# A kernel of spectral filter and gated MLP: two early activation columns moved ahead of the first weights, those weights in smaller loads and on two queues, and a row table moved back

## The chip, the cores and the metric

The kernel runs on one core of a Trainium2 chip. The metric is the device time of one execution in microseconds (us). A run of a kernel is repeated in rounds beside the kernel before on the same chip; medians are quoted. Ratios are computed as the mean time of one kernel's fast runs over that of the other's of the same rounds, so they are not quite the ratio of the medians quoted beside them. Brackets after a ratio hold its 95% interval. A core's execution can fall into a slower state.

Engine names in the profile: PE is TensorE's matmuls, PEld TensorE's weight loads, DVE VectorE, ACT ScalarE, POOL GpSimd, SPq and ACTq the queues of instructions on SyncE and ScalarE that issue loads (a load is moved afterwards by the core's 16 DMA engines).

## The reference

The output is the sum of the input, of a spectral filter of its layernorm, and of a gated MLP of the same layernorm:

```python
x = A_x                                    # 1 x 2048 x 512, bf16
xn = _layernorm(x, axis=-1)
# A: irfft2(rfft2(xn) * (w_r + 1j*w_i)), cast to bf16
# B: g = xn @ w_gate; u = xn @ w_up        # 512 x 1792 each
#    h = gelu_tanh(g) * u; h @ w_down      # 1792 x 512
return x + A(xn) + B(xn)
```

## The kernel before

The 2048 rows of x are 16 "columns" of 128 rows. TensorE needs x normalised and transposed (`xnT`), so column 0 must land, be normalised on VectorE, be transposed on TensorE and be copied out before the first gate matmul can run. Meanwhile TensorE runs dummy matmuls on a zero tile. The first gate and up matmuls work on columns 0 and 1 and on 512 of the 1792 weight columns (512 KB for each of `Wg_sb` and `Wu_sb`). All loads go out on SyncE in this order:

```python
pin(load_x(0, 1))                          # 128 KB, column 0
pin(load_x(1, 1))                          # 128 KB, column 1
nc.sync.dma_start(out=idx_t[:], ...)       # row table: 12 bytes to each partition, 1.5 KB
load_w(Wg_sb, 0, 512)                      # 512 KB, packets of 1 KB
load_w(Wu_sb, 0, 512)                      # 512 KB
load_x(2, 2)                               # 256 KB, packets of 2 KB
load_w(Wg_sb, 512, 1024)
load_w(Wu_sb, 512, 1024)
load_x(4, 2)
load_x(6, 2)
load_w(Wg_sb, 1024, DF)
load_w(Wu_sb, 1024, DF)
load_x(8, 2)
# [... more columns and constants]
for k in range(37):
    pin(nc.tensor.matmul(sp_ps[:, :P], lhsT=spin[:], rhs=spin[:], start=True, stop=True))
```

A list scheduler written in the kernel puts the rest in order, from guesses of when data lands. Its guesses touch the order of instructions only; the real waits are on semaphores.

```python
LAND = {0: 2.9, 1: 3.6, 2: 8.4, 3: 8.4}             # columns of x
WG_LAND = [6.3] * 4 + [10.2] * 4 + [13.2] * 6       # gate weights, by 128 columns
WU_LAND = [7.4] * 4 + [11.7] * 4 + [15.2] * 6
# [...]
# the first gate block, in two halves (rows 0-255 and 256-511 of the weights):
if k == 0:
    g = add("PE", occ / 2, lambda: mm_half(0), [xT_op[0, 0]], key=1000, acq=("G",), t_min=WG_LAND[0])
    g = add("PE", occ / 2, lambda: mm_half(1), [xT_op[0], g], key=1000.1, lat=occ / 2 + 0.3)
# [...]
u = split("u_ps", "U", Wu_sb, 1003.1 if k == 2 else 1000.5 + k, WU_LAND, (2, m, 1)[k] if k < 3 else m)
```

## Time and profile before

| | before |
|---|---|
| median time, us | 178.76 (178.62 to 179.22) |
| span of the profiled execution, us | 176.7 |
| TensorE busy in it, us | 171.1 (97%) |
| first gate matmul starts, us | 6.13 |
| first up matmul starts, us | 7.60 |
| third weight group starts (second gate group), us | 8.51 |

First two lines of the page: the busy time of each engine with its share of the span, and TensorE's busy tenths in 40 equal slices.

```profile
PE 171.1 (97%) x1127; PEld 96.2 (54%) x1145; DVE 116.1 (66%) x255; ACT 95.9 (54%) x170; POOL 17.2 (10%) x38
...
PE   7899999999999999999999999999999999999993
```

The busy time by stretch of the same kernel: the stretch, its length, then busy us and number of instructions of PE, PEld, DVE, ACT and POOL, the granted TensorE clock, the busy share of the DMA engines, and GB/s.

```profile
0.00:5.00 5.00, 3.62 (x38) 3.46 (x39) 2.10 (x10) 1.87 (x3) 0.69 (x6) 1.00 0.46 131
5.00:6.13 1.13, 0.85 (x10) 0.51 (x11) 1.07 (x5) 1.10 (x2) 0.00 (x0) 1.00 1.08 379
6.13:14.00 7.87, 7.68 (x106) 7.19 (x107) 4.71 (x12) 3.34 (x6) 0.97 (x2) 1.00 1.04 360
14.00:24.00 10.00, 9.95 (x80) 7.73 (x80) 9.82 (x24) 5.09 (x8) 1.73 (x4) 1.00 1.06 353
24.00:60.00 36.00, 35.79 (x218) 18.50 (x221) 24.06 (x44) 27.95 (x50) 13.81 (x26) 1.00 0.66 147
```

TensorE works without gaps of note from 7.6 us to the end, so an opening that is shorter by half a microsecond is half a microsecond won.

The opening, in the timeline: start, duration, engine, line, operation, tiles, shape, count of merged instructions, and in brackets the idle time before it with what ended it.

```profile
2.17 0.43 SPq L277 DMA_DIRECT2D Wg_sb<-in_B_w_gate_dram  x1
2.65 0.51 SPq L277 DMA_DIRECT2D Wu_sb<-in_B_w_up_dram  x1
2.96 0.69 DVE L339 BATCH_NORM_STATS2 stats<-x_t 128x6 f32<-128x512 bf16 x1 [1.94 <-DMA x_t<-in_A_x_dram]
...
5.59 0.29 DVE L354 COPY xnT<-tp 128x256 bf16<-128x256 bf16 x1
...
6.13 0.90 PEld L498 LDWEIGHTS <-Wg_sb 128*128 128x128 bf16 x16 [0.41 <-DMA Wg_sb<-in_B_w_gate_dram]
6.13 1.07 PE L498 MATMUL g_ps<-xnT,Wg_sb 128*128 128x128 bf16 x16 [0.24 <-DMA Wg_sb<-in_B_w_gate_dram]
...
7.60 1.07 PE L490 MATMUL u_ps<-xnT,Wu_sb 128*128 128x128 bf16 x16 [0.18 <-DMA Wu_sb<-in_B_w_up_dram]
...
8.51 1.06 PE L490 MATMUL g_ps<-xnT,Wg_sb 128*128 128x128 bf16 x16
```

Column 0 is ready at 5.88 (the copy at 5.59 takes 0.29), TensorE has done its last dummy matmuls at 5.89, and the gate matmul waits 0.24 us from there for its weights. The up matmul waits 0.18 for its own. So 0.4 us of waiting for loads can be seen, and that is what the change goes for.

### The profile page before, as it was taken

The numbers are of one execution on the slowest core, as the hardware profiler recorded it, in microseconds if no ns is written. First come the engines' busy times: TensorE is split into PE (matmuls) and PEld (weight loads), VectorE is DVE, ScalarE is ACT, GpSimd is POOL, SyncE is SP. The second block draws the span as 40 slices with busy tenths as digits, with TensorE's granted clock in tenths as the row PEclk, the third lists the DMA queues.
The fourth block names the chain that finished last, engine by engine and source line by source line (L and its number), as shares of the span: only waits on it lengthen the run. The fifth ranks groups of instructions, "written<-read, shape, count | busy, mean of one in ns | idle before, by whom it ended". The sixth has DMA issues, their size and how long they took to land.

```text
span 176.7 us, 3114 instructions
## 1 busy us (share of the span) xinstructions
PE 171.1 (97%) x1127; PEld 96.2 (54%) x1145; DVE 116.1 (66%) x255; ACT 95.9 (54%) x170; POOL 17.2 (10%) x38
## 2 busy tenths in 40 slices
PE   7899999999999999999999999999999999999993
PEld 7698845455544554555555445454444445444463
DVE  3588999987333699979899999643516325345333
ACT  4442489799736988898899965362112111211200
POOL 1020340506760000000000000000000000000000
PEclk9999999999999999999999999999999999999999
DMA  3999999234718702211211510200122221221212
GB/s 98 345 382 377 375 183 151 59 73 64 253 32 269 269 2 58 59 31 34 59 25 36 152 46 15 59 0 4 59 89 89 82 71 61 89 89 60 82 41 59
DMA packets 21871, 19.35 MB, mean 110 GB/s; under 512 B 8480, under 2 KB 20000, under 8 KB 21856
## 3 DMA queue, kind: packets, MB, share of 16 engines
q1 hardware_dynamic: 21440, 17.84, 36.2%
q0 software_dynamic: 416, 1.32, 2.4%
q8 instruction: 9, 0.15, 0.4%
q14 instruction: 6, 0.05, 0.1%
HBM read 13.38 MB, written 2.10 MB: 88 GB/s over the span
## 4 chain that ended last, share of the span: by engine, by line
PE 94%; DMA 3%; SPq 1%; issue 1%; DVE 0%
PE u_ps L490 27%; PE y_ps L817 27%; PE g_ps L490 27%; DMA Wu_sb<-in_B_w_up_dram 3%; PE yp L768 2%; PE gp L738 2%; PE bp L577 2%; PE dp L635 2%; PE y_ps L821 2%; PE ep L644 2%; SPq L273 0%; PE tp L351 0%; SPq L277 0%; SPq L284 0%; DVE y_sb L824 0%
## 5 line engine op out<-in xcount | busy, mean ns | idle before, releaser
L490 PE MATMUL u_ps<-xnT,Wu_sb 128*128 128x512 bf16 (+2 forms) x264 | 56.5, 340 | 0.5 <-DMA Wu_sb<-in_B_w_up_dram 0.2
L490 PE MATMUL g_ps<-xnT,Wg_sb 128*128 128x512 bf16 (+2 forms) x252 | 55.9, 349 | 0.2
L817 PE MATMUL y_ps<-Wd_sb,hT 128*128 128x512 bf16 (+2 forms) x246 | 50.6, 355 | 0.3
L508 DVE TENSOR_TENSOR hT<-u_ps,ge 128x512 bf16<-128x512 f32 x56 | 38.4, 688 | 18.1 <-PE u_ps L490 11.1
L503 ACT ACTIVATE ge<-g_ps 128x512 bf16<-128x512 f32 x56 | 33.7, 601 | 24.2 <-PE g_ps L490 20.8
L490 PEld LDWEIGHTS <-Wu_sb 128*128 128x128 bf16 x272 | 24.8, 98 | 21.0 <-DMA Wu_sb<-in_B_w_up_dram 0.4
L817 PEld LDWEIGHTS <-hT 128*128 128x128 bf16 x252 | 23.2, 98 | 22.4
L490 PEld LDWEIGHTS <-Wg_sb 128*128 128x128 bf16 x256 | 24.0, 98 | 20.6
L774 ACT CAST yf<-yp 128x512 bf16<-128x512 f32 x16 | 9.3, 586 | 40.5 <-PE yp L768 40.5
L824 DVE TENSOR_TENSOR y_sb<-y_ps,y_sb 128x512 bf16<-128x512 f32 (+2 forms) x18 | 11.1, 631 | 30.0 <-PE y_ps L821 30.0
L649 ACT CAST E<-ep 64x512 bf16<-64x512 f32 x32 | 18.5, 579 | 1.4 <-PE ep L644 1.0
L339 DVE BATCH_NORM_STATS2 stats<-x_t 128x6 f32<-128x512 bf16 x16 | 10.4, 674 | 2.6 <-DMA x_t<-in_A_x_dram 2.6
L452 ACT ACTIVATE xn<-x_t,nb,rstd 128x512 bf16<-128x512 bf16 x12 | 9.5, 812 | 1.0 <-POOL nb L370 1.0
L547 ACT CAST ds<-dp 128x512 bf16<-128x512 f32 x16 | 9.2, 597 | 0.8 <-PE dp L635 0.8
L547 ACT CAST Gs<-gp 128x512 bf16<-128x512 f32 x16 | 8.7, 591 | 0.6 <-PE gp L738 0.5
L547 ACT CAST Bs<-bp 128x512 bf16<-128x512 f32 x16 | 8.3, 608 | 0.5 <-PE u_ps L490 0.5
L780 DVE TENSOR_TENSOR lv<-yf 128x512 bf16<-128x512 bf16 x16 | 6.1, 422 | 1.5 <-ACT yf L774 0.6
L768 PEld LDWEIGHTS <-Gs 128*128 128x128 bf16 x64 | 4.8, 98 | 3.5
L787 DVE TENSOR_TENSOR yt<-lv 128x512 bf16<-128x512 bf16 x16 | 6.1, 422 | 0.3
L768 PE MATMUL yp<-CT,Gs 128*128 128x128 bf16 x64 | 6.0, 219 | 0.1
L821 PE MATMUL y_ps<-yt,RI_t 128*128 128x512 bf16 (+2 forms) x18 | 6.1, 355 | 0.0
L559 DVE TENSOR_TENSOR A<-xn 128x1024 bf16<-128x1024 bf16 x8 | 5.2, 676 | 1.0 <-ACT xn L452 1.0
(65 smaller groups left out, 118.2 us busy)
## 6 DMA issues: line engine op xcount, KB each, us to landing
F<-F SPq DMA_DIRECT2D x32, 64.0 KB, 2.0
y_sb<-in_A_x_dram SPq DMA_DIRECT2D x16, 128.0 KB, 2.1
out_dram<-y_sb SPq DMA_DIRECT2D x15, 128.0 KB, 1.7
x_t<-in_A_x_dram SPq DMA_DIRECT2D x7, 256.0 KB, 8.7
Wd_sb<-in_B_w_down_dram SPq DMA_DIRECT2D x1, 1792.0 KB, 7.7
Wg_sb<-in_B_w_gate_dram SPq DMA_DIRECT2D x2, 512.0 KB, 6.4
Wu_sb<-in_B_w_up_dram SPq DMA_DIRECT2D x2, 512.0 KB, 6.1
Wg_sb<-in_B_w_gate_dram SPq DMA_DIRECT2D x1, 768.0 KB, 10.2
```

Source lines behind the costliest of these rows:

```text
L339: V.bn_stats(out=st[:], in_=x_t[:, c, :])
L452: xn_op[c] = add("ACT", 0.72, lambda c=c: A.activation(out=xn[:, c, :], in_=x_t[:, c, :], func=AF.Identity, bias=nb[:, c:c + 1], scale=rst ...
L490: T_.matmul(b[name][:, f], lhsT=W_[:, e, (f0 + f) * P:(f0 + f + 1) * P], rhs=rhs[:, e, :], start=(e == 0), stop=(e == NE - 1))
L503: A.activation(out=b["ge"][:], in_=b["g_ps"][:], func=AF.Gelu_apprx_tanh)
L508: V.tensor_tensor(out=hT_of(sb, f0, m, o, w), in0=b["u_ps"][:], in1=b["ge"][:], op=ALU.mult)
L547: A.copy(out=o, in_=i)
L649: A.copy(out=b["E"][64 * h:64 * h + 64, r], in_=b["ep", h][64 * r:64 * r + 64])
L768: T_.matmul(t[:, q], lhsT=late["G"][:, q, c0 + j], rhs=IQ[q], start=(q == 0), stop=(q == 3), skip_group_check=True)
L774: A.copy(out=b["yf"][:, j], in_=b[j][:])
L817: T_.matmul(b[o][:], lhsT=hT_of(sb, f, 1, cl * P, P)[:, 0], rhs=Wd_sb[:, f, o:o + w], start=(f == 0), stop=False)
L821: T_.matmul(b[o][:], lhsT=late["RI"][:, c, :], rhs=late["yt"][:, c, o:o + w], start=False, stop=True)
L824: V.tensor_tensor(out=b["y"][:, o:o + w], in0=b[o][:], in1=b["y"][:, o:o + w], op=ALU.add)
```

## The change

The intent: bring columns 2 and 3 in while the weights would only start slowly; let two hardware queues feed the DMA engines with the first gate weights, in quarters, so that the first matmuls may start on a part; hold ScalarE's issues back behind a longer VectorE write to the same tile (a memset of zeros that the loads must wait for), so that they do not overtake column 0; move a tiny row table out of the front; use larger loads later on; and adapt the scheduler's guesses. The core of the diff (the rest moves the same statements into a function `opening()` that is called at the head of the schedule):

```diff
+        nc.vector.memset(Wg_sb[:, 0, 0:1536], 0.0)
 ...
-    nc.sync.dma_start(out=idx_t[:], in_=nc.inline_tensor(idx_np, name="spec_rows").ap())
-    load_w(Wg_sb, 0, 512)
-    load_w(Wu_sb, 0, 512)
-    load_x(2, 2)
+        load_x(2, 2)
+        for e in range(NE):
+            load_w(Wg_sb, 0, 512, nc.sync if e % 2 else nc.scalar, e=e)
+        load_w(Wu_sb, 0, 512, e=slice(0, 2))
+        load_w(Wu_sb, 0, 512, e=slice(2, 4))
 ...
-    load_x(4, 2)
-    load_x(6, 2)
+        load_x(4, 4)
 ...   # likewise columns 8-11 and 12-15; RF_t in one load; idx_t behind the columns
-    LAND = {0: 2.9, 1: 3.6, 2: 8.4, 3: 8.4}
-    WG_LAND = [6.3] * 4 + [10.2] * 4 + [13.2] * 6
-    WU_LAND = [7.4] * 4 + [11.7] * 4 + [15.2] * 6
+    LAND = {0: 2.9, 1: 3.6, 2: 7.2, 3: 7.2}
+    WG_LAND = [5.0] * 4 + [8.6] * 4 + [13.2] * 6
+    WU_LAND = [6.2] * 4 + [10.0] * 4 + [15.2] * 6
 ...   # statistics of columns 2-3 not before column 1's copy
-        u = split("u_ps", "U", Wu_sb, 1003.1 if k == 2 else 1000.5 + k, WU_LAND, (2, m, 1)[k] if k < 3 else m)
+        u = split("u_ps", "U", Wu_sb, 1000.5 + k, WU_LAND, (2, m, 1)[k] if k < 3 else m)
```

More of the change, by code (lines that the diff above doesn't have):

```diff
@@ L262 @@
     warm = pc.tile([P, 1], F32, name="warm")
-    nc.vector.memset(spin[:], 0.0)
-    nc.vector.memset(eps_t[:], EPS)
     minus_half = pc.tile([P, 4], F32, name="minus_half")
-    nc.vector.memset(minus_half[:], -0.5)
     ident_t = pc.tile([P, P], BF16, name="ident_t")
-    nc.gpsimd.memset(ident_t[:], 1.0)
-    nc.gpsimd.affine_select(out=ident_t[:], in_=ident_t[:], pattern=[[-1, P]], compare_op=ALU.is_equal, fill=0.0,
-                            base=0, channel_multiplier=1)
     def load_x(c0, n, eng=nc.sync):
@@ L277, in load_w @@
         return eng.dma_start(out=T[:, e, a:b], in_=v[:, e, a:b])
-    pin = tc.keep_in_program_order
-    pin(nc.scalar.activation(out=warm[:], in_=eps_t[:], func=AF.Sqrt, bias=eps_t[:], scale=1.0))
-    pin(load_x(0, 1))
-    pin(load_x(1, 1))
     idx_t = pc.tile([P, 3], I32, name="idx_t")
-    nc.sync.dma_start(out=idx_t[:], in_=nc.inline_tensor(idx_np, name="spec_rows").ap())
-    load_w(Wg_sb, 0, 512)
-    load_w(Wu_sb, 0, 512)
-    load_x(2, 2)
-    load_w(Wg_sb, 512, 1024)
-    load_w(Wu_sb, 512, 1024)
@@ L290 @@
-    load_x(4, 2)
-    load_x(6, 2)
-    load_w(Wg_sb, 1024, DF)
-    load_w(Wu_sb, 1024, DF)
-    load_x(8, 2)
-    load_x(10, 2)
-    for c in range(0, NC, 8):
-        nc.sync.dma_start(out=RF_t[:, c:c + 8], in_=rf_d.rearrange("p (c k) -> p c k", c=NC)[:, c:c + 8])
-    load_x(12, 2)
-    load_x(14, 2)
-    load_consts("F0", "L0")
-    load_consts("I0", "M0")
-    for T, w_in in ((TR, A_w_r), (TI, A_w_i)):
-        rows = w_in.rearrange("(kb a h g) k -> h kb a (g k)", kb=NC, h=2, a=8)
-        Tf = T.rearrange("p j k -> p (j k)")
-        for h in range(2):
-            nc.sync.dma_start(out=Tf[64 * h:64 * h + 64, W:8 * W], in_=rows[h, :, 0:4, W:8 * W])
@@ L308, with opening @@
-    LAND = {0: 2.9, 1: 3.6, 2: 8.4, 3: 8.4}
+    def opening():
+        nc.vector.memset(spin[:], 0.0)
+        nc.vector.memset(eps_t[:], EPS)
+        nc.vector.memset(minus_half[:], -0.5)
+        nc.vector.memset(Wg_sb[:, 0, 0:1536], 0.0)
+        U = nc.gpsimd
+        U.memset(ident_t[:], 1.0)
+        U.affine_select(out=ident_t[:], in_=ident_t[:], pattern=[[-1, P]], compare_op=ALU.is_equal, fill=0.0,
+                        base=0, channel_multiplier=1)
+        nc.scalar.activation(out=warm[:], in_=eps_t[:], func=AF.Sqrt, bias=eps_t[:], scale=1.0)
+        load_x(0, 1)
+        load_x(1, 1)
+        load_x(2, 2)
[3 more added lines that the diff above has]
+        load_w(Wu_sb, 0, 512, e=slice(2, 4))
+        load_w(Wg_sb, 512, 1024)
+        load_w(Wu_sb, 512, 1024)
+        load_x(4, 4)
+        load_w(Wg_sb, 1024, DF)
+        load_w(Wu_sb, 1024, DF)
+        load_x(8, 4)
+        nc.sync.dma_start(out=RF_t[:], in_=rf_d.rearrange("p (c k) -> p c k", c=NC))
+        load_x(12, 4)
+        nc.sync.dma_start(out=idx_t[:], in_=nc.inline_tensor(idx_np, name="spec_rows").ap())
+        load_consts("F0", "L0")
+        load_consts("I0", "M0")
+        for T, w_in in ((TR, A_w_r), (TI, A_w_i)):
+            rows = w_in.rearrange("(kb a h g) k -> h kb a (g k)", kb=NC, h=2, a=8)
+            Tf = T.rearrange("p j k -> p (j k)")
+            for h in range(2):
+                nc.sync.dma_start(out=Tf[64 * h:64 * h + 64, W:8 * W], in_=rows[h, :, 0:4, W:8 * W])
+        for k in range(37):
+            nc.tensor.matmul(sp_ps[:, :P], lhsT=spin[:], rhs=spin[:], start=True, stop=True)
@@ L318 @@
     sp_ps = ps.tile([P, D], F32, name="sp_ps", tag="S", bufs=4)
-    for k in range(37):
-        pin(nc.tensor.matmul(sp_ps[:, :P], lhsT=spin[:], rhs=spin[:], start=True, stop=True))
     def spin_on():
@@ L427, in first_two, with moments @@
         xn_op[1] = o["xn1"]
+        return o["copyt"]
     ROOT = 1.1
-    first_two()
-    def moments(c, key):
-        s = add("DVE", 0.6, lambda: f_stats(c), key=key, t_min=LAND[c] if c < 4 else max(LAND[c], 14.7))
+    chain_end = first_two()
+    def moments(c, key, after=None):
+        s = add("DVE", 0.6, lambda: f_stats(c), key=key, t_min=LAND[c] if c < 4 else max(LAND[c], 14.7), after=after)
         return add("DVE", 0.1, lambda: f_mean(c), [s], key=key - 0.5)
     def second_two():
-        m = [moments(c, -1200 + c) for c in (2, 3)]
+        m = [moments(c, -1200 + c, chain_end) for c in (2, 3)]
         m = add("POOL", ROOT, lambda: root_eps(2, 2), m, key=-1190, lat=ROOT + 0.1)
@@ L848 @@
     with tc.manual_schedule(engines={E_.PE, E_.DVE, E_.Activation, E_.Pool, E_.SP}):
+        opening()
         for op in plan.order():
```

## The prediction

> **What bounds the kernel now.** TensorE. The page gives PE 171.1 of 176.7 us busy. The table of busy times by stretch shows PE 5.00 us of the first 5 (dummy warm-up matmuls), 0.85 of 5.00-6.13, 7.68 of the next 7.87, and over 99% from 14 us to the end of the matmuls. Only the opening can be shortened by moving loads; what is won there goes through to the end, because PE has no later slack that would swallow it.
>
> **The opening, before** (timeline, list of waits):
> - Column 0's transposes run at 4.95 us and the copies to xnT end at 5.56 and 5.88. The first gate matmul could start at about 5.6, but starts at 6.13: the weight load waited 0.41 us for the DMA of Wg_sb, issued at 2.17.
> - Transposes of column 1 run 7.04-7.43; the first up matmul starts at 7.60: it waited for Wu_sb (0.35 us on the weight load, 0.18 on PE). The chain of waits runs through this DMA (2.65 to 7.56).
> - After 7.60 PE has no wait of note.
>
> By the packet records, columns 0 and 1 move at about 260 GB/s, then come the 12-byte packets of the row table, then Wg starts slowly (about 120 GB/s for 1 us) before the engines reach 380.
>
> **What the change does.**
> 1. The row table leaves the front; it is not read before 41 us (gathers on POOL): free.
> 2. Columns 2-3 (256 KB) go ahead of the weights: 0.7 us at 380 GB/s in front of Wg, but it fills the slow start. Their transposes run at 12 us, off the path.
> 3. Wg's first 512 KB in quarters, two from ScalarE's queue, so that two queues feed the engines while SP still issues (0.43 us an issue). The Trainium skill, "DMA: Bandwidth & Descriptors", section "Issuing engines are not separate DMA queues", says that such DMAs interleave on the same 16 engines and only issue time is saved; this trace, with one queue, cannot show it. The first half of the gate matmuls can start with two quarters.
> 4. The VectorE memset of 768 words: 64 words took 0.11 us and one 0.06, so an estimate of 0.6 to 0.9 us, ending near 1.8. VectorE waits for x until 2.96, so it is free; it holds ScalarE's first load back behind x.
> 5. PE's sequence: the up matmuls of the first 256-wide unit now come before the transposes of columns 2-3, so the second up block is needed near 10.5 instead of 12.49. It landed at 11.3 before. Later a few small groups swap places; same work.
>
> **Estimate.** From 256 KB landed at 3.4 us, at 375 GB/s: Wg complete near 5.5, Wu 7.0, second Wg block 8.5-9, second Wu block 10-10.5. First gate matmul 5.6 instead of 6.13 (held by the copy to xnT); transposes end at 6.9; first up matmul 7.0 instead of 7.60. Gain 0.6 us, of which 0 to 0.2 may return as a wait for the second Wu block. Net 0.55: 178.8 to 178.25 us; 8 in 10 between 177.6 and 178.9. Faster by over 2% (3.6 us) is impossible with at most 1.5 us of recoverable idle.
>
> **What would show it.** First gate matmul within 0.15 us of 5.6, released by VectorE, not DMA; first up matmul at 6.9-7.2; column 2-3 statistics right after column 1's copy, near 7.3 instead of 8.55; PE without waits at 9.5-11; PE's busy time unchanged.
>
> **What would make it wrong.** ScalarE's load issues queue behind SP's and delay its square root at 3.90; ScalarE's data delays column 0; the warm-up matmuls wait for the long memset, so the first transposes start late; the slow start stays with the weights and Wg lands at 6 again; the second Wu block is late by 0.5 us.

## The result, and the profile after

| | before | after |
|---|---|---|
| median of 4 runs each, us | 178.76 (178.62 to 179.22) | 179.94 (179.72 to 180.10) |
| ratio | | 1.0061 [1.0039, 1.0082] |
| span of the profiled execution, us | 176.7 | 178.4 |
| granted clock | 1.000 | 1.000 |
| first gate matmul, us | 6.13 | 6.70 |
| first up matmul, us | 7.60 | 8.35, most of the group 9.11 |
| third weight group, us | 8.51 | 9.90 |

The change is within 2%, but it makes the kernel 0.6% slower where 0.3% faster was predicted. The page of the kernel after, its first two lines and the line of the queue that is new:

```profile
PE 172.4 (97%) x1127; PEld 96.9 (54%) x1145; DVE 116.5 (65%) x256; ACT 95.7 (54%) x170; POOL 17.6 (10%) x38
...
PE   7899999999999999999999999999999999999993
...
q10 hardware_dynamic: 288, 0.26, 0.5%
```

The same 1127 matmuls, one more VectorE instruction (the memset), and 0.26 MB on a second hardware queue. The opening in the timeline of the kernel after:

```profile
1.12 0.70 DVE L278 MEMSET Wg_sb<- 128x768 uint32 x1
1.85 0.38 ACTq L270 DMA_DIRECT2D Wg_sb<-in_B_w_gate_dram  x1
2.17 0.91 SPq L270 DMA_DIRECT2D Wg_sb<-in_B_w_gate_dram  x2
...
3.30 0.69 DVE L338 BATCH_NORM_STATS2 stats<-x_t 128x6 f32<-128x512 bf16 x1 [1.48 <-DMA x_t<-in_A_x_dram]
...
6.04 0.29 DVE L353 COPY xnT<-tp 128x256 bf16<-128x256 bf16 x1
...
6.69 0.75 PEld L498 LDWEIGHTS <-Wg_sb 128*128 128x128 bf16 x12 [0.51 <-DMA Wg_sb<-in_B_w_gate_dram]
6.70 1.30 PE L498 MATMUL g_ps<-xnT,Wg_sb 128*128 128x128 bf16 x16 [0.34 <-DVE xn L344]
...
7.60 0.23 PEld L498 LDWEIGHTS <-Wg_sb 128*128 128x128 bf16 x4 [0.16 <-DMA Wg_sb<-in_B_w_gate_dram]
...
8.35 0.28 PE L490 MATMUL u_ps<-xnT,Wu_sb 128*128 128x128 bf16 x2
...
9.11 0.96 PE L490 MATMUL u_ps<-xnT,Wu_sb 128*128 128x128 bf16 x14 [0.48 <-DMA Wu_sb<-in_B_w_up_dram]
...
9.90 1.06 PE L490 MATMUL g_ps<-xnT,Wg_sb 128*128 128x128 bf16 x16
```

The memset and ScalarE's issues came as planned. The gate weights did not. The last quarter of `Wg_sb` let four weight loads run only at 7.60, and the second half of `Wu_sb` came at 9.11. By the third weight group TensorE is 9.90 - 8.51 = 1.39 us behind.

That lag then stays constant to 40 us. A second loss follows in the matmuls `bp` of the spectral part, the third of four groups. Timeline of the kernel before, these matmuls alone:

```profile
35.93 1.06 PE L577 MATMUL bp<-RF_t,xf 128*128 128x128 bf16 x16
39.41 1.06 PE L577 MATMUL bp<-RF_t,xf 128*128 128x128 bf16 x16
```

The same of the kernel after:

```profile
37.32 1.06 PE L577 MATMUL bp<-RF_t,xf 128*128 128x128 bf16 x16
40.80 1.37 PE L577 MATMUL bp<-RF_t,xf 128*128 128x128 bf16 x16
```

37.32 - 35.93 = 1.39 and 40.80 - 39.41 = 1.39: nothing lost or won between. The group at 40.80 takes 0.31 longer, and 1.39 + 0.31 = 1.70 is the whole difference of the two spans. The medians are only 1.18 apart: the profiled execution of the kernel after is the slowest of its four (180.10), and that of the kernel before took 178.40. The two traces show about 0.5 us more than the change costs.

### Did the DMA engines move less?

No. Adding up the sizes of the trace's packet records (not a view of the profile) gives the time, from the start of the span, at which so many KB had been moved in all:

| KB moved | 256 | 512 | 768 | 1024 | 1280 | 1536 | 2048 |
|---|---|---|---|---|---|---|---|
| before, us | 3.09 | 4.71 | 5.39 | 6.08 | 6.80 | 7.60 | 9.26 |
| after, us | 3.04 | 4.41 | 5.23 | 5.97 | 6.68 | 7.38 | 8.81 |

After is a little ahead everywhere. But in the kernel before, columns 0-1 and `Wg_sb`'s block are the first 768 KB (5.39 us); in the kernel after, columns 2-3 stand in front of it as well and it is the first 1024 KB (5.97). That explains 0.58 us. The rest is another thing: the last piece of `Wg_sb` could be used at 7.60, 1.6 us after as many bytes as it needs had been moved; the last of `Wu_sb` at 9.11, 1.7 us after 7.38. In the kernel before these delays are 6.13 - 5.39 = 0.7 and 7.60 - 6.80 = 0.8. The Trainium skill, "DMA: Bandwidth & Descriptors", section "Why a DMA increments its semaphore by 16 and not by 1", says that a load is carried by up to 16 DMA engines that finish independently, and that only the full count means that all data landed. So one DMA engine that is behind delays the load, whatever the other fifteen have moved. The trace agrees: it keeps the time of each of a load's 16 increments (read from the kept trace, not a view of the profile).

```
increments of one load's semaphore, us    8th    15th   16th
before, first block of Wg_sb              5.79   6.03   6.09
before, first block of Wu_sb              7.27   7.49   7.56
after, columns 2-3                        4.70   5.25   6.45
after, last quarter of Wg_sb              6.21   6.67   7.56
after, second half of Wu_sb               7.75   8.15   9.06
```

From the eighth increment to the last it is 1.3 us for these weights in the kernel after and 0.3 in the kernel before. In the kernel after the last increment comes alone: 0.7 to 1.2 us after the fifteenth, for columns 2-3 and for each of the seven weight loads that follow. So a late last share is what the matmuls waited for in this execution; that is shown. What makes it late is not. One packet of columns 2-3 took 972 ns where 84 is the median of their size, but the packet records do not name their engine, so that packet cannot be tied to the late share.

Nor is such a lag peculiar to the kernel after. For the first block of `Wu_sb` it is 0.3 to 0.4 us in the profiled executions of the kernel before, e7 and e16 (the experiments follow below), but 0.9 to 1.1 in those of e5, e11 and e13, which load this block whole, on one queue and ahead of columns 2-3, as the kernel before does.

### The profile page after: what moved, and what is told of

Its sections match the earlier page's. It is cut to its first block, busy times and chain, and to the rows that moved or that the text cites. A ratio compares the mean times of both kernels' runs of the same rounds, so it can differ in the third digit from the quotient of the medians.

```text
span 178.4 us, 3115 instructions
## 1 busy us (share of the span) xinstructions
PE 172.4 (97%) x1127; PEld 96.9 (54%) x1145; DVE 116.5 (65%) x256; ACT 95.7 (54%) x170; POOL 17.6 (10%) x38
## 4 chain that ended last, share of the span: by engine, by line
PE 89%; DMA 3%; ACT 2%; DVE 2%; SPq 1%; issue 1%
PE y_ps L817 27%; PE u_ps L490 25%; PE g_ps L490 25%; DMA Wu_sb<-in_B_w_up_dram 3%; PE dp L635 2%; PE yp L768 2%; PE gp L738 2%; PE y_ps L821 2%; PE ep L644 2%; PE bp L577 1%; ACT Bs L547 1%; DVE hT L508 1%; SPq L270 1%; SPq L266 1%; DVE A L559 1%
## 5 line engine op out<-in xcount | busy, mean ns | idle before, releaser
L644 PE MATMUL ep<-ds,CT 128*128 128x512 bf16 x16 | 5.9, 379 | 0.0
```

The lines of the kernel that those rows point to most:

```text
L644: T_.matmul(t[:], lhsT=cc("L" if g + h else "L0"), rhs=b["ds", h][:], start=True, stop=True)
```

## The experiments

Eighteen kernels ran. All gave the reference's result. Three theories stood at first: **A**, columns 2-3 in front of the weights cost the time; **B**, the second hardware queue does; **C**, the packets of 2 KB of columns 2-3 hold up the packets of 1 KB of the weights. **D** came with them: the time lies in the instruction order, not in the loads.

### Round 1: undo one part of the change (kernel before in the same rounds: 178.66)

**e1_one_queue**: the kernel after with all four gate quarters on SyncE.

```diff
-            load_w(Wg_sb, 0, 512, nc.sync if e % 2 else nc.scalar, e=e)
+            load_w(Wg_sb, 0, 512, e=e)
```

> The changed kernel with all four Wg quarters issued by SP; nothing from ScalarE's queue. Theory A (columns 2-3 in front of the weights are the cost: one DMA engine is late with them and everything behind it in that engine's queue is late too): still slow, first gate matmul 6.3-6.8 us, up matmuls not running freely before 8.3, time 179.4-180.3. Theory B (two queues interleaving are the cost): first gate matmul back at 5.6-6.2, up matmuls by 7.6, column 0's statistics back at 2.96, time 178.0-178.9.

Measured: 180.40, ratio 1.0098 [1.0082, 1.0114]. It is slower than the kernel after, not faster. TensorE's matmuls and weight loads in this run:

```profile
5.72 1.13 PE L498 MATMUL g_ps<-xnT,Wg_sb 128*128 128x128 bf16 x12
...
6.45 0.23 PEld L498 LDWEIGHTS <-Wg_sb 128*128 128x128 bf16 x4 [0.30 <-DMA Wg_sb<-in_B_w_gate_dram]
...
7.56 0.40 PE L498 MATMUL g_ps<-xnT,Wg_sb 128*128 128x128 bf16 x4 [0.71 <-DMA Wg_sb<-in_B_w_gate_dram]
```

Two quarters were there by 5.72; the weight loads of the third started at 6.45 and those of the fourth only at 7.56, in the order of one queue. Theory B falls.

**e2_cols_behind**: the kernel after with `load_x(2, 2)` moved behind the two halves of `Wu_sb`.

> The changed kernel with columns 2-3 issued after the first Wu halves, ScalarE's quarters kept. Theory A: most of the loss goes: first gate matmul by 6.1, up matmuls flowing by 7.7, time 178.4-179.2 (the 0.3 us stall near 41 us may remain, as it is one of the order on ScalarE). Theory B: still 179.4-180.3.

Measured: 179.94 (179.06 to 180.60), 1.0064 [1.0038, 1.0089]: nothing regained. The gate began at 6.27 without a wait, but the second half of `Wu_sb` came at 8.57 after a wait of 0.57, and the second block of `Wu_sb` was waited for at 12.85 (0.44). Theory A alone misses: with the columns out of the way, the pieces of weights still come late.

**e3_cols_split**: the kernel after with columns 2 and 3 as two loads (packets of 1 KB).

> The changed kernel with columns 2 and 3 loaded as two one-column loads, in place, so that their packets are 1 KB, not 2 KB. Theory C (the 2 KB packets, which took up to 0.97 us each here, are what leaves an engine late): first gate matmul by 6.1, up by 7.7, time 178.4-179.2. Theories A and B: no better than the changed kernel, 179.4-180.3.

Measured: 181.27 (179.89 to 183.0, one of six runs slow; the median of the fast ones is 181.14), 1.0122 [1.0095, 1.0148]. Worse. Theory C falls.

**e4_before_cols_ahead**: the kernel before with only `load_x(2, 2)` moved in front of the row table and the weights.

> The kernel before with one move alone: columns 2-3 issued ahead of the row table and Wg, all else as before, the same order on all engines. Theory A: slower than before by 0.6-1.4 us, Wg landing at 6.6 or later, Wu at 8.2 or later. Theory B: within 0.5 us of before, Wg landing later by the 0.3-0.7 us that 256 KB take.

Measured: 181.53, 1.0166 [1.0141, 1.0190]. This one move, on whole loads and one queue, costs far more than the whole change, and more than the 0.6 to 1.4 us that theory A allowed. TensorE in its timeline:

```profile
7.97 1.59 PE L498 MATMUL g_ps<-xnT,Wg_sb 128*128 128x128 bf16 x16 [2.04 <-DMA Wg_sb<-in_B_w_gate_dram]
9.90 1.89 PE L490 MATMUL u_ps<-xnT,Wu_sb 128*128 128x128 bf16 x16
```

And two stretches of it (columns as above; the eighth entry, ahead of the last two, is the granted clock):

```profile
7.90:12.00 4.10, 4.03 (x42) 3.85 (x43) 1.93 (x6) 0.60 (x1) 0.05 (x1) 0.58 1.08 372
12.00:16.00 4.00, 4.00 (x57) 3.79 (x55) 2.08 (x5) 1.79 (x4) 0.92 (x2) 1.00 1.06 375
```

In this execution, after a wait of 2.04 us, TensorE's clock was granted at 0.58 on the mean for some 4 us, and groups of 16 matmuls took 1.59 and 1.89 us instead of 1.07. So the wait was paid for twice. It is not the whole cost: one of the five runs of e4 kept a mean clock of 1.000 and still took 180.86. In the kernel after the clock is 1.000.

### Round 2: order against loads (before: 178.66)

**e5_order_only**: the kernel before with the new landing guesses, the new place of the third up group and the opening function; loads as before.

> The changed kernel's order on PE, VectorE and ScalarE with the loads of the kernel before (one queue, whole blocks, columns 2-3 behind Wu). If the loss is in the loads (theory A, or its successor A2: single packets that stall for 0.3 to 1.1 us early on leave one DMA engine late, and every load behind waits for that engine): the opening is as before (gate 6.13, up 7.60), and only the order's share shows: a short wait of 0.1-0.3 us for the second up block near 11.2 and the 0.3 us stall near 41 us; 178.8-179.4. If the order were the main cause: 179.6-180.3.

Measured: 179.00, 1.0017 [1.0000, 1.0034], in the range for loads as the cause. Two things expected did not come. The third `bp` group is not slow (1.06), and the opening of the profiled execution (179.24) is not as before, though the loads are:

```profile
6.94 1.07 PE L499 MATMUL g_ps<-xnT,Wg_sb 128*128 128x128 bf16 x16 [0.60 <-DMA Wg_sb<-in_B_w_gate_dram]
8.34 1.07 PE L491 MATMUL u_ps<-xnT,Wu_sb 128*128 128x128 bf16 x16
```

With the same loads in the same order, the gate starts 0.81 and the up matmuls 0.74 us later than in the trace of the kernel before. So the late share that theory A2 supposes is seen with the old loads too: from the eighth increment to the last it is 1.0 us for `Wu_sb`.

**e6_loads_only**: the kernel after with the old guesses and keys, so the old order.

```diff
-    LAND = {0: 2.9, 1: 3.6, 2: 7.2, 3: 7.2}
+    LAND = {0: 2.9, 1: 3.6, 2: 8.4, 3: 8.4}
 ...   # WG_LAND, WU_LAND, chain_end and the key of the third up group as before
```

> The changed kernel's loads with the order of the kernel before on all compute engines. Loads as the main cause: first gate 6.3-6.8 and free-running up matmuls at 8.5-9.2 as in the changed kernel, no stall near 41 us: 179.3-180.0. Order as the main cause: 178.5-179.0.

Measured: 179.71, 1.0056 [1.0043, 1.0069]; gate 6.86, up 8.63 and 9.41, as late as in the kernel after, and the same slow `bp` group (1.38 us), which was not expected here. Theory D falls for most of the loss: the loads carry it.

**e7_table_late**: the kernel before with the row table's load moved behind the columns of x, and nothing else.

> The kernel before with the row table's load moved behind the x columns, nothing else. If the 12-byte packets cost the weights their 0.3 us in the queue: Wg lands at 5.7-5.9, gate matmul then too, 178.2-178.6. If the slow start of the third load is there whatever it is: same as before within 0.15 us, 178.5-178.9. Slower than 179.2 would mean that the early stalls depend on the mix of loads in ways neither theory tells.

Measured: 178.24 (178.02 to 178.69), 0.9982 [0.9967, 0.9997]. TensorE in its timeline:

```profile
6.00 1.06 PE L498 MATMUL g_ps<-xnT,Wg_sb 128*128 128x128 bf16 x16
7.34 1.07 PE L490 MATMUL u_ps<-xnT,Wu_sb 128*128 128x128 bf16 x16
```

0.13 and 0.26 us earlier than before, and no wait for weights shown. By the two ratios (this one and e13's, 0.18% and 0.21% of 178.7) a table of 1.5 KB in front of the weights cost 0.3 to 0.4 us. This is the part of the change that works.

**e8_scalar_later**: the kernel after with the memset done twice, so that ScalarE issues its loads later still (2.77 instead of 1.85 us).

> The changed kernel with the VectorE memset done twice, so that ScalarE issues its quarters from about 2.6 us instead of 1.85. If ScalarE's issues while column 0 is in flight are what makes column 0 land late (its statistics began at 3.13-3.30 in all three runs with ScalarE issues so far, at 2.95-3.00 in all without): statistics at 2.95-3.0, first transposes at 4.97. If not: 3.1-3.3 again. Time 179.4-180.4 either way, as the up weights still gate.

Measured: 180.06, 1.0080 [1.0066, 1.0093]. Column 0's statistics began at 3.56, not earlier; over all runs this start varies from 2.95 to 3.56 whatever ScalarE does (3.41 in e5, which has no ScalarE load). The theory that ScalarE's loads delay column 0 falls.

### Round 3: one part alone (before: 178.72)

The base of the next kernels is e7's loads, written in the opening function.

**e9_quarters**: base, with the gate quarters on both queues and the memset.

```diff
+        nc.vector.memset(Wg_sb[:, 0, 0:1536], 0.0)
-        load_w(Wg_sb, 0, 512)
+        for e in range(NE):
+            load_w(Wg_sb, 0, 512, nc.sync if e % 2 else nc.scalar, e=e)
```

> Base for these four: the kernel before with the row table late (178.24 in the last run). Added here: Wg's first block in quarters on both queues, with the memset. Theory Q (cutting the first weights into more loads makes the last piece land later, as the run with columns 2-3 behind was still at 179.94): 178.9-179.6, Wg complete or Wu landing 0.5-1 us later than with whole blocks. If quarters are harmless: 177.9-178.5.

Measured: 180.08, 1.0070 [1.0053, 1.0088], above the range of theory Q. Its timeline:

```profile
5.81 1.06 PE L501 MATMUL g_ps<-xnT,Wg_sb 128*128 128x128 bf16 x16
8.21 1.07 PE L493 MATMUL u_ps<-xnT,Wu_sb 128*128 128x128 bf16 x16 [1.13 <-DMA Wu_sb<-in_B_w_up_dram]
```

The gate weights were in time; it is the *next* load, still in one piece, that came late. The stretches show what was missing, in this run: kernel e9,

```profile
6.00:7.00 1.00, 1.00 (x20) 0.91 (x17) 0.33 (x2) 0.79 (x2) 0.00 (x0) 1.00 0.80 238
7.00:8.00 1.00, 0.09 (x2) 0.00 (x0) 0.42 (x1) 0.50 (x1) 0.00 (x0) 1.00 0.77 219
```

and e7, which differs from it by the quarters and the memset:

```profile
6.00:7.00 1.00, 1.00 (x22) 1.00 (x19) 0.47 (x2) 0.88 (x1) 0.00 (x0) 1.00 1.08 370
7.00:8.00 1.00, 0.93 (x17) 0.76 (x15) 0.42 (x1) 0.60 (x1) 0.00 (x0) 1.00 1.01 277
```

The last two entries: the DMA engines were busy 0.80 and 0.77 of the time and moved 238 and 219 GB/s, against 370 and 277. Of the 16 increments for `Wu_sb` the eighth came at 6.82 and the last two at 8.06 and 8.17; in e7 these are 6.98, 7.25 and 7.30. So half of the DMA engines were in time and some were late.

**e10_up_halves**: base with `Wu_sb`'s first block in two halves by rows, both on SyncE.

> The same base, Wu's first block in two halves on SP, nothing else. Theory Q: 178.5-179.1. If halves are harmless: 178.0-178.5.

Measured: 179.22, in two clusters (three runs at 178.59 to 178.90, three at 179.55 to 179.78), 1.0018 [0.9996, 1.0039]: above both expectations, but with no change inside the interval.

**e11_fours**: base with columns 4 to 15 in loads of four and `RF_t` in one.

> The same base, columns 4-15 in three loads of four (4 KB packets) and RF in one, nothing else. If the bigger loads are part of the loss (later weights are issued earlier and compete): 178.6-179.2, by a later second Wg or Wu block. If not: 178.0-178.5.

Measured: 178.91, 1.0005 [0.9988, 1.0022]: in the range for a loss, but with no change from the kernel before inside the interval.

**e12_cols_ahead**: base with columns 2-3 in front of the weights.

> The same base, columns 2-3 ahead of Wg, nothing else. Theory A: 256 KB in front of the weights cost at least their 0.7 us at 380 GB/s, in the earlier run with the row table in front even 2.9 us: 179.2-181.0, first gate matmul at 6.6 or later. If that 2.9 us came from the row table between columns and weights: below 179.2.

Measured: 179.86, 1.0072 [1.0051, 1.0093].

```profile
7.56 1.07 PE L499 MATMUL g_ps<-xnT,Wg_sb 128*128 128x128 bf16 x16 [1.19 <-DMA Wg_sb<-in_B_w_gate_dram]
```

So theory A is half right: columns ahead do cost 1.6 us when they are the only fault. They just are not the only fault in the kernel after. A wait of 1.19 us left the mean clock of this execution at 1.000, where e4's 2.04 did not; in another of the six runs of e12 (180.75, not profiled) the mean clock was 0.988.

### Round 4: what about a cut costs (before: 178.67)

**N** says that the number of loads in flight costs, **R** that a load by row blocks, whose packets interleave from several places, does.

**e13_table_late_again**: base, to be sure of e7.

> The kernel before with the row table late, once more, as the base of this call: 178.0-178.6, ratio to before 0.996-0.9995.

Measured: 178.47, 0.9979 [0.9963, 0.9994]. Confirmed by the times. The trace warns, though: in this execution (178.74) the same kernel's first gate matmul starts at 6.48, in e7's (178.11) at 6.00. One execution's opening can differ by half a microsecond from another's; a trace shows where the time of its own execution went.

**e14_up_partition_halves**: base with `Wu_sb`'s first block in two loads of 64 partitions.

> The base with Wu's first block in two loads of 64 partitions each, which keep the order of rows within a partition. Theory N (number of loads): as the halves by rows, 178.5-179.2. Theory R (order of the rows read): as the base, 178.0-178.6.

Measured: 179.90, 1.0072 [1.0050, 1.0093]; `Wu_sb` at 8.70 after a wait of 1.20. The engines were busy over 100% of 6 to 8 us and moved only 228 and 216 GB/s: packets were slower. The time is above both expectations. This kernel cannot tell N from R, because cutting by partitions brought a fault of its own.

**e15_up_quarters**: base with `Wu_sb`'s first block in four quarters on SyncE.

> The base with Wu's first block in four loads of 128 rows on SP. Both theories: slower than the halves, 179.2-180.2, with Wu landing 0.5-1 us later than in the base or the second Wg block late. If it is no slower than 178.6, cutting Wu is harmless and the 179.22 of the halves was chance.

Measured: 178.74 (178.54 to 179.69), 1.0005 [0.9983, 1.0027], less than I expected. N falls as a general rule: four loads for one are nearly free at this place.

**e16_order_table_late**: base with the kernel after's order.

> The changed kernel's order on PE, VectorE and ScalarE with the base's loads. If the order by itself costs a wait for the second up block, needed near 10.9 and landing near 11.0: 178.2-178.8, up to 0.4 us over the base. If the order is neutral: within 0.15 us of the base.

Measured: 178.70, 1.0000 [0.9986, 1.0015]: about 0.2% above e13, with intervals that overlap. In its trace the second part of the third up group starts at 11.30 where 11.12 would have done: the wait for the second `Wu_sb` block that the prediction allowed for, 0.18 us.

### Round 5: queue or cut (before: 178.46)

**e17_quarters_one_queue**: base, gate quarters all on SyncE, no memset.

> The base (row table late) with Wg's first block in quarters, all on SP; no memset, nothing on ScalarE's queue. If the second queue is the cost: near the base, 178.3-178.9. If the cut of Wg is the cost: 179.5-180.5, Wg's quarters early but Wu landing after 8.0.

Measured: 180.00 (179.24 to 180.40), 1.0092 [1.0078, 1.0106]. (Its profiled run is the luckiest of five, 179.24, so its trace understates the loss.)

**e18_halves_two_queues**: base, gate weights in two halves, one on ScalarE's queue behind the memset.

> The base with Wg's first block in two halves of 256 rows, one on ScalarE's queue behind the memset, one on SP's. If the second queue is the cost: 179.5-180.3, as the quarters on both queues. If the cut is: about half of their loss, 178.9-179.5.

Measured: 178.88 (178.80 to 179.02), 1.0024 [1.0010, 1.0037], at the lower end of the range for the cut. In its trace 0.31 us are the slow `bp` group, so the halves themselves cost less than the table below says; the same holds for the 0.9% of e9.

The Trainium skill, "DMA: Bandwidth & Descriptors", section "Issuing engines are not separate DMA queues", says that a second issuing engine saves only issue time. These runs agree: quarters cost 0.9% above base on two queues (1.0070 over 0.998) and 1.1% on one (1.0092 over 0.998). The second queue is neither the gain that the change hoped for nor the fault; the cut of the first gate load in four is.

### The parts together

Over base, whose ratio to before is 0.998:

| one part alone | over base |
|---|---|
| gate quarters, two queues, memset (e9) | +0.9% |
| gate quarters, one queue (e17) | +1.1% |
| gate halves, two queues, memset (e18) | +0.4% |
| columns 2-3 ahead (e12) | +0.9% |
| up halves by rows (e10) | +0.4% |
| later loads in fours (e11) | +0.2% |
| order (e16) | +0.2% |
| the whole change | +0.8% |

The parts (e9, e12, e10, e11 and e16) add up to 2.6%, the change has 0.8%. Probably they do not add because they mostly make the same thing late: weights for the first 10 us. That would also explain why undoing one of them (e1, e2, e6) regained nothing or little. The small entries are unsure: e10, e11 and e16 have no change from the kernel before inside their intervals, and the base's own interval is 0.15% to either side.

### The slow group at 41 us

Seven kernels show the third `bp` group at 1.37 us or nearly so: after, e1, e2, e3, e6, e9 and e18. These are exactly those with the memset once. The kernel before and the other twelve experiments (eleven without that memset, and e8 with two) have 1.06 to 1.08. In the seven, VectorE starts one and the same write of `hT` late; timeline of the kernel after:

```profile
26.75 0.69 DVE L508 TENSOR_TENSOR hT<-u_ps,ge 128x512 bf16<-128x512 f32 x1 [0.65 <-ACT xn L452]
```

and the same write in the kernel before:

```profile
24.95 0.69 DVE L508 TENSOR_TENSOR hT<-u_ps,ge 128x512 bf16<-128x512 f32 x1 [0.24 <-PE u_ps L490]
```

The write needs an up group and a gelu, which had ended at 26.23 and 26.01 in the kernel after. The profile names ScalarE's `xn`, ended at 26.70. In the built program the instruction does not wait for it: its waits are for the same ScalarE and TensorE instructions as in e8, which has no delay. Yet in all seven kernels it starts 36 to 48 ns after that `xn` ends, which is too regular for chance. The delay of about 0.4 us passes on through the statistics, `xn` and the copies of `bp`. What makes this one instruction late is open. That it goes with the memset is a correlation over all kernels, without a mechanism. Whether a second memset takes it away is less sure than the list says: e8's profiled run took 179.10 us, 0.9 less than the fastest of its other five, so its trace may not show its usual course.

### Best version

e7 (and e13, the same loads): 178.24 and 178.47 us against 178.66 and 178.67 of the kernel before in the same rounds. It beats both kernels, the kernel before by 0.2%. It keeps the kernel before and moves one line: the row table's load behind the columns.

## Why the prediction was wrong, point by point

- **Bound by TensorE, opening goes through to the end: right.** The lag at 9.90 us is still 1.39 at 40.80.
- **The step that failed:** "From 256 KB landed at 3.4 us, at 375 GB/s: Wg complete near 5.5, Wu 7.0". It took the landing of a load for bytes over rate, from 3.4 us on. The last increments came at 7.56 for `Wg_sb` and at 9.06 for `Wu_sb`, 2.1 us late each. Two terms of the sum were wrong:
  - *The fill.* "It fills the slow start" did not make the start fast. The 256 KB from 256 to 512 were moved from 3.04 to 4.41 us, in 1.37 us, with columns 2-3 in that place, against an assumed 0.7. `Wg_sb`'s share of the bytes was in at 5.97, 0.58 us later than before, where the forecast had it 0.6 earlier (5.5 against 6.13). The slow start is not something that the weights have and columns do not: these 256 KB took 1.62 us in the kernel before, and 0.91 to 1.54 in the eighteen experiments, whichever load stood there. e12 shows the price of the columns by themselves: gate at 7.56.
  - *The last piece.* From the eighth of the 16 increments to the last it was 1.3 us for `Wg_sb` and `Wu_sb`, against 0.3 before. The forecast had no term for a DMA engine that falls behind. Cutting the load does not shorten it: each quarter has its own 16 increments, and is as late as the latest of them.
- **"The first half of the gate matmuls can start with two quarters": of no use.** In the kernel after the group started at 6.70 and its last weights came at 7.60; in e1 two quarters were in time and the fourth held the group until 7.56. TensorE took its matmuls in the program's order (the transposes of column 1, at 7.79 in e1, stood behind the fourth quarter): what counted was the last quarter.
- **"First gate matmul within 0.15 us of 5.6, released by VectorE, not DMA": wrong**, 6.70 and by the load (the profile puts the matmul's wait down to VectorE, which wrote `xn` long before; its weight load waited for the DMA until 6.69). Part of this is no fault of the change: column 0's statistics began at 3.30 in this execution and at 2.96 in the one before, which moved the copies to `xnT` from 5.56 and 5.88 to 6.00 and 6.33. And 5.6 was too early in any case: the last dummy matmuls stand ahead in TensorE's order until 5.89 in the kernel before, and the earliest gate start of any run is 5.72 (e1). "First up matmul at 6.9-7.2": wrong, 8.35 and 9.11. "Column 2-3 statistics near 7.3": wrong, 8.60.
- **The memset "0.6 to 0.9 us, ending near 1.8": right**, 0.70, ending at 1.82. "It is free": not shown. It went with a loss of 0.31 us at 41 us that no one could have read from the trace before.
- **Row table "free": right as a cost, without the gain.** The move cost nothing, but the forecast gave it no gain of its own, and it was worth 0.3 to 0.4 us (e7, e13). The packet reading that the prediction itself reported ("then come the 12-byte packets of the row table, then Wg starts slowly") pointed there.
- **Order: a little undersized.** "0 to 0.2 may return as a wait for the second Wu block": that wait is 0.18 in e16, but the medians give 179.00 - 178.66 = 0.34 us in e5 and 178.70 - 178.47 = 0.23 in e16 over e13, the first with an interval that touches no change.
- **Of the things that "would make it wrong"**, "the slow start stays with the weights and Wg lands at 6 again" is nearest. ScalarE's issues delaying column 0 was tested and fell (e8, e5).

What stays open: why the cut of the first gate load costs 0.9% to 1.1%, while the same cut of the up load just behind it costs 0.2% to 0.3% over base, with intervals that overlap (e15); and what makes the last share late. Packets that took over 200 ns more than their kind does are found in every kernel in 3 to 10 us: 11 before (the worst by 440 ns), 24 after (888), but also 23 in e7, which is fastest. So their number does not explain the time; where they fall, and how much of a needed load is behind them, may. That is argued, not shown.

## What to carry to other kernels

A load has landed when the last DMA engine's share is in, so a forecast for a load that the critical path waits for needs, besides bytes over rate, a term for this last piece, taken from the trace (here 0.3 us from the eighth DMA engine to the last in the kernel before, 1.3 after, and 0.3 to 1.1 in single executions of kernels with whole loads in the old place). Keep what is needed first in front and in one load; cutting 512 KB in quarters so as to start on a part bought nothing here, since the matmuls behind the last quarter stood behind it in TensorE's order, and it came as late as the whole, or later. Moving a load of 12-byte packets from in front of a needed one was worth 0.3 to 0.4 us here, and a change with several parts is worth testing part by part: the one that paid was the one thought to be free.

## What the Trainium skill lacked or had wrong

- "DMA: Bandwidth & Descriptors", "Rules for kernel authors", advises to coalesce small transfers and puts the limit of mostly overhead at 64 KB. Here quarters of 128 KB in place of a load of 512 KB cost 0.9% to 1.1% of the kernel (e9, e17), and halves of 256 KB up to 0.4% (e10, whose interval includes no change, and e18, whose trace has 0.31 us of another cause), though each is above that limit. Quarters of the next load cost only 0.2% to 0.3% (e15).
- The same section says of two loads to disjoint partition halves that they gain nothing. Here they were worse than nothing: +0.9% over base (e14), with the DMA engines fully busy at 216 to 228 GB/s.
- No page says how far apart in time the 16 DMA engines may finish one load. Here the last of the 16 increments came 0.3 us after the eighth in the kernel before and 1.3 us in the kernel after, and a single packet took 972 ns in place of 84.
- No page says what a load of 12 bytes to each of 128 partitions costs the loads behind it: 0.3 to 0.4 us here (e7, e13).
- "TensorE: Matmul & The Clock Gate", "Part 1: The HAM clock gate (the "warmup" mystery)", speaks of an idle window of about 3.4 us before the clock drops. In e4 a wait of 2.04 us was followed by a granted clock of 0.58 on the mean from 7.9 to 12 us; a wait of 1.19 us (e12) was not. These are single executions, and no run here shows what decides.
